# Column norms of one batch by a wide product, and ten output pairs stored singly

## The chip, the cores and the metric

The kernel runs on one core of one Trainium2 (trn2) chip. The metric is device time in microseconds (us) of one execution, as the median of several runs. The core has a matrix engine (TensorE, called PE in the profile, with its weight loads as PEld), VectorE (DVE), ScalarE (ACT), GpSimd (POOL) and a queue engine (SyncE, SP), beside sixteen DMA engines that move data between the chip's large memory (HBM) and the on-chip memory. Products of TensorE are written to PSUM, a small memory of banks that hold 512 floats in each of 128 partitions.

## The reference

There are four batches of 6400 tokens with 256 channels. In each batch the columns of q and k are scaled to length one over the tokens, a 256x256 matrix of attention between channels is formed, and v is multiplied by it. A mixture of eight rank-16 adapters with the best two per token is added to the result.

```python
def _attn_ref(q, k, v, tau):                      # q, k, v: (4, 6400, 256) float32
    qn = q / (np.linalg.norm(q, axis=1, keepdims=True) + 1e-06)
    kn = k / (np.linalg.norm(k, axis=1, keepdims=True) + 1e-06)
    s = kn.transpose(0, 2, 1) @ qn / tau
    s = s - s.max(-1, keepdims=True)
    a = np.exp(s)
    a /= a.sum(-1, keepdims=True) + 1e-09
    return v @ a

def _moe_ref(x, w_gate, A, B):                    # x: (25600, 256), 8 experts of rank 16
    logits = x @ w_gate
    topk = np.argpartition(-logits, 2, axis=1)[:, :2]
    sel = np.take_along_axis(logits, topk, axis=1)
    w = softmax(sel)                              # written out in the reference
    for e in range(8):
        for k in range(2):
            mask = topk[:, k] == e
            delta[mask] += w[mask, k, None] * (x[mask] @ A[e] @ B[e])
    return x + delta
```

## The kernel before

Each batch is cut into 50 chunks of 128 tokens, which lie in the partitions; partition p holds tokens 50p to 50p+49. q and k of a batch arrive in five stripes of ten chunks (tile `qk`, four buffers), v in stripes of 18, 16 and 16 chunks (tile `vt`, three buffers). The loads of q, k and v are issued from POOL's queue and change float32 to bfloat16 on the way; the first four chunks of q and k come through SP as float32 instead and are cast on VectorE and ScalarE. `load_more` issues the loads in one fixed order, each as soon as its buffer has been read to the end.

For a chunk, `gram` (L201) adds k-transposed times q to the bank `acc` by two products of 128x128 weights with 256 moving columns. `square` (L189) writes the squares of q and k of two chunks to a tile `sq` of 2x2x256 bfloat16 (four buffers), on ScalarE, or in batch 0 on VectorE and ScalarE in turn. `norm` (L212) sums the squares over the tokens with TensorE: for each of four blocks of 128 channels (two of q, two of k) the squares are loaded as weights and multiplied by one column of ones, so that the sums land in four columns of the bank `nrm`, one channel in each partition.

When a batch's chunks are through, `chain0` to `chain6` make its matrices: Ln and Exp on ScalarE for the root of the sums (`chain0`), the reciprocal and diagonal matrices on VectorE, a product with ones that spreads q's scales over the partitions, the product with `acc`, the exponential, transposes, and the small matrices `wa` (gate and adapters A, multiplied by the attention) and `a`.

The output is made in pairs of chunks, 25 in a batch, 100 in all (numbers u from 0): transposes of v (L341), gate logits for a group of pairs (L362), the gating steps on VectorE, the adapter products (`z_gz`, L447), `y_mm` (L463), transposes of the gated values (L471), and `delta` (L480), which adds the adapters' part (L483) and copies the pair to the tile `ys` on ScalarE (L487). A group is five pairs (the last two groups of batch 3 are three and two).

The order is written out by hand. First all of batch 0's norms and matrices; its loop takes two chunks a step, and the norms run four chunks behind the products of `gram`. All its chain steps are emitted before the first transposes of v. Then comes a loop over slots, each with one pair's work and, up to slot 67, with two or three chunks of a later batch. Stores of `ys` go out by whole groups (10 KB in a partition, 1.31 MB) and are held back: `send` keeps up to six finished groups and issues the others from ScalarE's queue, or from SP's when none is to be kept, from slot 91 on. The last five pairs are stored one by one from SP (2 KB in a partition), as the lines of `delta` say:

```python
        if u >= NPT - GRP:
            c0 = 2 * (u % NPAIR)
            nc.sync.dma_start(out_v[gr["b"], :, c0:c0 + 2, :], gr["ys"][:, r["w"]:r["w"] + 2, :])
        elif u == gr["f"] + gr["n"] - 1:
            unsent.append(gr)
```

with NPT = 100 and GRP = 5.

Of the kernel before, what the change touches and what calls it, by code (L numbers as in the profile page):

```python
# [8 lines left out]
FP32 = mybir.dt.float32  # L9
BF16 = mybir.dt.bfloat16  # L10
AX = mybir.AxisListType
OP = mybir.AluOpType
ACT = mybir.ActivationFunctionType
# [3 lines left out]
def kernel(  # L17
# [16 lines left out]
    nc = tc.nc  # L34
    B, N, C = q.shape
    P = 128
    NC = N // P
# [9 lines left out]
    NPT = B * NPAIR  # L47
    GRP = 5
# [13 lines left out]
    const = ctx.enter_context(tc.tile_pool(name="const", bufs=1))  # L62
    qk_pool = ctx.enter_context(tc.tile_pool(name="qkp", bufs=QKB))
    v_pool = ctx.enter_context(tc.tile_pool(name="vp", bufs=VB))
    sq_pool = ctx.enter_context(tc.tile_pool(name="sqp", bufs=4))
# [54 lines left out]
    def load_more(limit=1000):  # L120

        while limit and at_load[0] < len(loads):
            _, kind, b, s, parts = loads[at_load[0]]
            n = len(left[kind])
            if n >= bufs[kind] and left[kind][n - bufs[kind]]:
                return
            where[kind, b, s] = n
            c0 = s * PC if kind == "qk" else sum(VP[:s])
            left[kind].append(PC if kind == "qk" else sum(parts))
            o = left[kind][-1] - sum(parts)  # L130
            if kind == "qk":
                t = qk_pool.tile([P, 2, PC, C], BF16, tag="qk", name="qk")
            else:
                t = v_pool.tile([P, max(VP), C], BF16, tag="v", name="vt")
            tiles[kind][b, s] = t
            for m in parts:
                if kind == "qk":
                    nc.gpsimd.dma_start(t[:, 0, o:o + m, :], q_v[b, :, c0 + o:c0 + o + m, :])  # L138
                    nc.gpsimd.dma_start(t[:, 1, o:o + m, :], k_v[b, :, c0 + o:c0 + o + m, :])
                else:  # L140
                    nc.gpsimd.dma_start(t[:, o:o + m, :], v_v[b, :, c0 + o:c0 + o + m, :])
                o += m
            at_load[0] += 1
            limit -= 1
# [11 lines left out]
    nc.sync.dma_start(bst, moe_B.rearrange("e r d -> (e r) d"))  # L156
    nc.sync.dma_start(ast, moe_A.rearrange("e (p cc) r -> p e (cc r)", p=P))
    load_more(3)
    ones_bf = const.tile([P, 2], BF16)
    nc.vector.memset(ones_bf, 1.0)  # L160
    ones_f = const.tile([P, P], FP32)
    nc.vector.memset(ones_f, 1.0)
# [9 lines left out]
    ident_f = const.tile([P, P], FP32)  # L172
# [14 lines left out]
    acc, nrm, sqs = {}, {}, {}  # L187
# [24 lines left out]
    def norm(b, c):  # L212
        if c == 0:
            nrm[b] = ps_nrm.tile([P, 512], FP32, tag="nrm", name="nrm")
        sq = sqs[b, c - c % 2]
        for w in range(2):
            for ic in range(CC):
                j = w * CC + ic
                nc.tensor.matmul(  # L219
                    nrm[b][:, j:j + 1], sq[:, w, c % 2, ic * P:(ic + 1) * P], ones_bf[:, 0:1],  # L220
                    start=(c == 0 and j == 0), stop=(c == NC - 1), skip_group_check=True)
# [3 lines left out]

    def chain0(b):
        d = st.setdefault(b, {})
        lnn = bat.tile([P, 4], FP32, name="lnn")
        nc.scalar.activation(lnn, nrm[b][:, 0:4], ACT.Ln)
        rt = bat.tile([P, 4], FP32, name="rt")  # L230
        nc.scalar.activation(rt, lnn, ACT.Exp, scale=0.5)
        d["rt"] = rt
# [71 lines left out]
    def chain6(b):  # L304
        d = st[b]
        a_bf = bat.tile([P, CC, C], BF16, name="a_bf")
        for ic in range(CC):
# [3 lines left out]


    CHAIN = [(chain0, 0.0), (chain1, 0.9), (chain2, 0.75), (chain3, 0.0), (chain4, 0.55),
             (chain5, 0.65), (chain6, 0.5)]

# [164 lines left out]
    def delta(u):  # L480
        r, gr = pr.pop(u), groups[u]
        for sc in range(2):
            nc.tensor.matmul(r["y"][:, sc, :], r["gzT"][:, sc, :], ball_sb, start=False,  # L483
                             stop=(sc == 1), skip_group_check=True)
        if "ys" not in gr:
            gr["ys"] = y_pool.tile([P, 2 * GRP, C], FP32, tag="ys", name="ys")
        nc.scalar.copy(gr["ys"][:, r["w"]:r["w"] + 2, :], r["y"])  # L487
        if u >= NPT - GRP:
            c0 = 2 * (u % NPAIR)
            nc.sync.dma_start(out_v[gr["b"], :, c0:c0 + 2, :], gr["ys"][:, r["w"]:r["w"] + 2, :])  # L490
        elif u == gr["f"] + gr["n"] - 1:
            unsent.append(gr)
# [11 lines left out]
    for c in range(0, NC, 2):  # L504
        square(0, c, "act" if (c // 2) % 2 else "dve")
        gram(0, c)
        gram(0, c + 1)
        load_more()
        if c >= 4:
            norm(0, c - 4)  # L510
            norm(0, c - 3)
    for c in range(NC - 4, NC):
        norm(0, c)
# [30 lines left out]
    zq, dq = None, None  # L544
    while nz < NPT or zq is not None or dq is not None:
# [10 lines left out]
        if f in (chain0, chain1, chain2, chain3):  # L556
            f(fb)
        u = None
        if nz < min(slot, NPT) and groups[nz]["ready"]:
            u = nz  # L560
# [9 lines left out]
        if dq is not None:  # L570
            delta(dq)
        dq, zq = zq, u
# [55 lines left out]
```

## Time and profile before

| what | value |
|---|---|
| median of 3 runs (lowest, highest) | 257.0 us (256.7, 257.05) |
| the profiled execution, its own time | 256.87 us |
| its span, first to last instruction | 255.1 us |
| TensorE matmul busy | 221.0 us (87%), 3256 matmuls |
| ScalarE busy | 176.5 us (69%) |
| VectorE busy | 151.2 us (59%) |
| norm products L219 | 800, 166 ns mean of one |
| read from HBM, written to it | 78.91 MB, 26.21 MB: 412 GB/s over the span |
| clock granted to TensorE, mean over the span | 0.964 |

In a group's row the number after x is a count; then come busy time and the mean duration of one. Matmuls are pipelined, so the mean of one is longer than the distance between two. In the row of tenths a digit is the busy share of one fortieth of the span (6.4 us). In the windows the columns are the stretch, its length, busy time and count for TensorE, weight loads, VectorE, ScalarE and GpSimd, the granted clock, the mean share of the sixteen DMA engines in use, and GB/s as the DMA records count them (a load that changes float32 to bfloat16 is counted by what it writes). A bracket at the end of a timeline row is the engine's idle time before it and what ended that.

### The profile page before, as it was taken

Reading aid. Unit: us, or ns where it says so; the run is one execution under the profiler, and the core shown is the slowest. Engines: PE = TensorE matmul, PEld = TensorE weight load, DVE = VectorE, ACT = ScalarE, POOL = GpSimd, SP = SyncE. Lnnn points to the kernel's source line nnn. Section 1 sums busy time; section 2 is a strip of 40 time slices with the busy share of each in tenths; the row PEclk is TensorE's granted clock in tenths of the full one; section 3 lists DMA queues with packets and bytes.
Section 4 is the critical chain, followed back from the end, with each engine's and each line's share of the span. In section 5 each row is a group of like instructions: output and inputs, shape, how many; then the busy total and the mean of one; then the engine's idle time right before and its main releaser. Section 6 shows DMA issues by size and latency. Waiting matters only on the chain.

```text
span 255.1 us, 7688 instructions
## 1 busy us (share of the span) xinstructions
PE 221.0 (87%) x3256; PEld 194.4 (76%) x3256; DVE 151.2 (59%) x575; ACT 176.5 (69%) x290; POOL 31.6 (12%) x64
## 2 busy tenths in 40 slices
PE   0758794785899999999999989999899899999991
PEld 0546582574799987998999878989898689999980
DVE  1322244235386686775867858666577687777760
ACT  3434346448178878887788796888776867787881
POOL 8131221021012010211101202000000100000000
PEclk9999998589599999999999999999999999999999
DMA  7999999999999999999999999999999999999985
GB/s 213 223 217 217 210 216 222 208 215 216 213 221 209 216 216 214 219 211 216 216 218 211 271 277 294 220 304 260 284 259 273 372 337 351 377 423 424 418 372 226
DMA packets 13170, 66.82 MB, mean 262 GB/s; under 512 B 2512, under 2 KB 2640, under 8 KB 9296
## 3 DMA queue, kind: packets, MB, share of 16 engines
q0 software_dynamic: 8064, 38.80, 74.3%
q10 hardware_dynamic: 2160, 19.66, 18.8%
q1 hardware_dynamic: 2912, 7.87, 8.4%
q8 instruction: 25, 0.41, 0.6%
q14 instruction: 9, 0.07, 0.1%
HBM read 78.91 MB, written 26.21 MB: 412 GB/s over the span
## 4 chain that ended last, share of the span: by engine, by line
PE 48%; DMA 36%; DVE 7%; ACT 3%; POOL 2%; issue 2%; DVEq 0%; ACTq 0%; POOLq 0%
DMA qk<-in_k_dram 20%; PE y_ps L463 12%; DMA vt<-in_v_dram 11%; PE acc L207 8%; PE zg L447 6%; PE y_ps L483 6%; DMA out_dram<-ys 5%; PE vT_ps L341 5%; PE zg L471 3%; PE vT_ps L362 3%; PE nrm L219 3%; ACT sq L197 2%; DVE gz L451 2%; POOL qk L138 1%; ACT ys L487 1%
## 5 line engine op out<-in xcount | busy, mean ns | idle before, releaser
L197 ACT ACTIVATE sq<-qk 128x1024 bf16<-128x1024 bf16 x87 | 89.7, 1055 | 25.9 <-DMA qk<-in_k_dram 17.5
L207 PE MATMUL acc<-qk 128*128 128x256 bf16 x400 | 81.5, 310 | 15.2 <-DMA qk<-in_k_dram 8.8
L487 ACT COPY ys<-y_ps 128x512 f32<-128x512 f32 x100 | 58.8, 588 | 26.2 <-PE y_ps L483 22.3
L463 PE MATMUL y_ps<-a_bf,vT 128*128 128x256 bf16 x400 | 60.3, 273 | 0.9 <-ACT ys L487 0.9
L219 PEld LDWEIGHTS <-sq 128*128 128x128 bf16 x800 | 46.9, 102 | 10.1 <-ACT sq L197 3.2
L451 DVE TENSOR_TENSOR gz<-zg,gate 128x256 bf16<-128x256 f32 x100 | 41.7, 418 | 14.4 <-PE zg L447 13.0
L207 PEld LDWEIGHTS <-qk 128*128 128x128 bf16 x400 | 34.6, 106 | 20.3 <-DMA qk<-in_k_dram 10.0
L352 DVE COPY vT<-vT_ps 128x512 bf16<-128x512 bf16 x63 | 26.7, 424 | 33.2 <-PE vT_ps L341 32.5
L219 PE MATMUL nrm<-ones_bf,sq 128*128 128x1 bf16 x800 | 45.2, 166 | 1.2 <-ACT sq L197 1.2
L341 PE MATMUL vT_ps<-ident,vt 128*128 128x128 bf16 x400 | 39.8, 224 | 5.1 <-DMA vt<-in_v_dram 5.0
L447 PE MATMUL zg<-wa_sb,vT 128*128 128x128 bf16 x400 | 38.5, 219 | 1.2 <-DVE gzT L477 1.0
L483 PE MATMUL y_ps<-ball_sb,gzT 128*128 128x256 bf16 x200 | 38.4, 274 | 0.0
L463 PEld LDWEIGHTS <-vT 128*128 128x128 bf16 x400 | 33.6, 97 | 3.8 <-issue 1.0
L341 PEld LDWEIGHTS <-vt 128*128 128x128 bf16 x400 | 30.3, 100 | 8.0 <-DMA vt<-in_v_dram 5.6
L350 ACT COPY vT<-vT_ps 128x512 bf16<-128x512 bf16 x37 | 21.8, 588 | 10.2 <-PE vT_ps L341 8.7
L471 PE MATMUL zg<-ident,gz 128*128 128x128 bf16 x200 | 27.7, 220 | 1.1 <-DVE gz L451 0.6
L447 PEld LDWEIGHTS <-vT 128*128 128x128 bf16 x400 | 26.0, 97 | 3.3 <-issue 2.2
L138 POOL DMA_DIRECT2D qk<-in_q_dram x21 | 11.4, 545 | 113.7 <-ACT sq L197 31.6
L477 DVE COPY gzT<-zg 128x256 bf16<-128x256 bf16 x90 | 25.3, 281 | 0.0
L199 DVE TENSOR_TENSOR sq<-qk 128x1024 bf16<-128x1024 bf16 x13 | 9.0, 691 | 23.6 <-DMA qk<-in_k_dram 13.5
L471 PEld LDWEIGHTS <-gz 128*128 128x128 bf16 x200 | 15.2, 98 | 2.9 <-DVE gz L451 2.5
L483 PEld LDWEIGHTS <-gzT 128*128 128x128 bf16 x200 | 16.2, 98 | 0.4
(56 smaller groups left out, 152.6 us busy)
## 6 DMA issues: line engine op xcount, KB each, us to landing
out_dram<-ys ACTq DMA_DIRECT2D x15, 1280.0 KB, 12.8
qk<-in_q_dram POOLq DMA_DIRECT2D x18, 640.0 KB, 20.2
qk<-in_k_dram POOLq DMA_DIRECT2D x18, 640.0 KB, 23.6
vt<-in_v_dram POOLq DMA_DIRECT2D x7, 1024.0 KB, 27.8
out_dram<-ys SPq DMA_DIRECT2D x4, 1280.0 KB, 8.9
vt<-in_v_dram POOLq DMA_DIRECT2D x4, 1152.0 KB, 24.0
out_dram<-ys SPq DMA_DIRECT2D x5, 256.0 KB, 4.9
qk<-in_q_dram POOLq DMA_DIRECT2D x2, 384.0 KB, 12.0
```

Of the source, the lines that this page charges most:

```text
L197: nc.scalar.activation(sq, src, ACT.Square)
L207: nc.tensor.matmul(acc[b][:, ic, :], t[:, 1, o, ic * P:(ic + 1) * P], t[:, 0, o, :], start=(c == 0 and ic == 0), stop=(c == NC - 1), skip_ ...
L219: nc.tensor.matmul(nrm[b][:, j:j + 1], sq[:, w, c % 2, ic * P:(ic + 1) * P], ones_bf[:, 0:1], start=(c == 0 and j == 0), stop=(c == NC - 1 ...
L341: nc.tensor.matmul(pt[:, ic, sc * P:(sc + 1) * P], vt[:, o + sc, ic * P:(ic + 1) * P], ident, is_transpose=True, start=(i == 0), stop=(i = ...
L352: nc.vector.tensor_copy(dst, src)
L447: nc.tensor.matmul(z[:, sc, :], r["vT"][:, ic, sc, :], st[b]["wa"][:, ic, E:E + ER], start=(sc == 0 and ic == 0), stop=(sc == 1 and ic == ...
L451: nc.vector.tensor_tensor(out=gz.rearrange("p c (e r) -> p c e r", e=E), in0=z.rearrange("p c (e r) -> p c e r", e=E), in1=gr["gate"][:, r ...
L463: nc.tensor.matmul(y[:, sc, :], r["vT"][:, ic, sc, :], st[b]["a"][:, ic, :], start=(sc == 0 and ic == 0), stop=False, skip_group_check=True)
L471: nc.tensor.matmul(gt[:, sc, :], r["gz"][:, sc, :], ident, is_transpose=True, start=(sc == 0), stop=(sc == 1))
L477: nc.vector.tensor_copy(gzT, gt)
L483: nc.tensor.matmul(r["y"][:, sc, :], r["gzT"][:, sc, :], ball_sb, start=False, stop=(sc == 1), skip_group_check=True)
L487: nc.scalar.copy(gr["ys"][:, r["w"]:r["w"] + 2, :], r["y"])
```

## The change

The column of ones becomes a 128x128 tile. For batch 0 alone, `norm` uses it as the weights and streams all 512 squares of a chunk (q's 256 columns and k's 256) in one product, 50 products instead of 200. Every partition of `nrm` then holds the sums of all 512 channels. To bring them to one channel in each partition, `chain0` multiplies the bank by the identity on VectorE (the result goes to a buffer from the pool of squares) and adds up each row of 128; Ln reads these four sums. The other batches keep the four narrow products. Apart from that, pairs 90 to 94 are stored singly from SP, as 95 to 99 were before.

```diff
-    ones_bf = const.tile([P, 2], BF16)
+    ones_bf = const.tile([P, P], BF16)
     nc.vector.memset(ones_bf, 1.0)
...
         sq = sqs[b, c - c % 2]
+        if b == 0:
+
+            nc.tensor.matmul(nrm[b].rearrange("p (w d) -> p w d", w=2), ones_bf, sq[:, :, c % 2, :],
+                             start=(c == 0), stop=(c == NC - 1))
+            return
         for w in range(2):
             for ic in range(CC):
                 j = w * CC + ic
...
     def chain0(b):
         d = st.setdefault(b, {})
+        sums = nrm[b][:, 0:4]
+        if b == 0:
+            dq = sq_pool.tile([P, 4 * C], BF16, tag="sq", name="dq").bitcast(FP32).rearrange(
+                "p (j d) -> p j d", j=4)
+            nc.vector.tensor_tensor(out=dq, in0=nrm[b].rearrange("p (j d) -> p j d", j=4),
+                                    in1=ident_f[:, None, :].to_broadcast([P, 4, P]), op=OP.mult)
+            sums = const.tile([P, 4], FP32, name="sums")
+            nc.vector.tensor_reduce(out=sums, in_=dq, axis=AX.X, op=OP.add)
         lnn = bat.tile([P, 4], FP32, name="lnn")
-        nc.scalar.activation(lnn, nrm[b][:, 0:4], ACT.Ln)
+        nc.scalar.activation(lnn, sums, ACT.Ln)
...
-        if u >= NPT - GRP:
+        if u >= NPT - 2 * GRP:
             c0 = 2 * (u % NPAIR)
             nc.sync.dma_start(out_v[gr["b"], :, c0:c0 + 2, :], gr["ys"][:, r["w"]:r["w"] + 2, :])
```

## The prediction

> **What bounds the kernel now.** I read the page first (busy tenths, clock, DMA), then the chain of waits, the timeline of TensorE up to 65 us, and last the end of the span in short windows.
>
> ```profile
> span 255.1 us, 7688 instructions
> ...
> PEclk9999998589599999999999999999999999999999
> DMA  7999999999999999999999999999999999999985
> ...
> q8 instruction: 25, 0.41, 0.6%
> ```
>
> The sixteen DMA engines are at 9 tenths or more in every slice but the first and the last two: the kernel moves a fixed 105.1 MB (78.9 read, 26.2 written) and is paced by that. Slices 7 to 9 show the clock lowered. The q8 line, 25 packets, is TensorE's instruction stream, loaded through the same engines; it decides the end, as shown below.
>
> ```profile
> 5.02 24.33 DMA qk<-in_k_dram
> 36.27 28.20 DMA vt<-in_v_dram
> ...
> 184.91 13.68 DMA out_dram<-ys
> ...
> 249.62 0.59 ACT ys L487
> ```
>
> These are pieces of the chain (start, length): twice in the first 65 us it goes through a transfer that waits over 20 us in a full queue, and the last compute step is a copy at 249.6. After it only stores are left.
>
> ```profile
> 30.48 1.01 PE L207 MATMUL acc<-qk 128*128 128x256 bf16 x4
> 31.29 0.40 PE L219 MATMUL nrm<-ones_bf,sq 128*128 128x1 bf16 x8
> 31.55 1.01 PE L207 MATMUL acc<-qk 128*128 128x256 bf16 x4
> ...
> 37.04 0.60 PE L207 MATMUL acc<-qk 128*128 128x256 bf16 x4
> 37.47 0.34 PE L219 MATMUL nrm<-ones_bf,sq 128*128 128x1 bf16 x8
> 37.68 0.60 PE L207 MATMUL acc<-qk 128*128 128x256 bf16 x4
> ...
> 47.31 0.61 PE L341 MATMUL vT_ps<-ident,vt 128*128 128x128 bf16 x4 [1.88 <-DMA vt<-in_v_dram]
> ...
> 54.15 0.39 PE L207 MATMUL acc<-qk 128*128 128x256 bf16 x2 [1.01 <-DMA qk<-in_k_dram]
> ...
> 64.52 0.61 PE L341 MATMUL vT_ps<-ident,vt 128*128 128x128 bf16 x4 [3.11 <-DMA vt<-in_v_dram]
> ```
>
> A pair of chunks of batch 0 takes 31.55 - 30.48 = 1.07 us until 35 us and 37.68 - 37.04 = 0.64 after: TensorE is at half clock at first. The brackets are its waits for data: 1.88 us before the first transpose, 1.01, then 3.11; with one of 0.39 at 59.67 that is 4.5 us of waiting behind 47.3 and 6.4 in all.
>
> ```profile
> 240.00:244.00 4.00, 4.00 (x51) 3.73 (x49) 3.01 (x14) 3.42 (x10) 0.00 (x0) 1.00 0.99 411
> 244.00:246.00 2.00, 2.00 (x25) 1.83 (x23) 1.21 (x7) 1.74 (x6) 0.00 (x0) 1.00 0.67 282
> 246.00:250.00 4.00, 3.25 (x32) 2.33 (x30) 1.49 (x6) 3.16 (x9) 0.00 (x0) 1.00 0.96 392
> 250.00:252.50 2.50, 0.00 (x0) 0.00 (x0) 0.00 (x0) 0.21 (x1) 0.00 (x0) 1.00 0.99 381
> 252.50:255.10 2.60, 0.00 (x0) 0.00 (x0) 0.00 (x0) 0.00 (x0) 0.00 (x0) 0.79 0.04 16
> ```
>
> The last two numbers are DMA share and GB/s. At 244 to 246 a third of the engines idle; after 252.5 the share is 0.04 of sixteen, less than one engine. Each transfer leaves sixteen completion marks in the trace, one per engine. The last store: fifteen marks at 252.79 to 253.02, one at 254.01. The lone engine is late in all five last stores and in the two before them (249.78 against 250.90 for pairs 90 to 94, 246.73 against 247.85 for 85 to 89). Its cause is in the packet records: a q8 packet of 16 KB holds one engine for 0.88 to 0.98 us. After the first (22.5 us) one of the sixteen marks falls 0.8 us behind its neighbours, after the second (36.1) a second one, and so on to eight by 102 us; the ninth packet (107.4) puts one of those eight 2.5 us behind the first, and then the next ones. So the packets go round eight engines. Packet 25, at 243.0, is the fourth for the engine that had the 1st, 9th and 17th; the seven others have three. Marks carry no engine numbers, so it is an inference that the engines without any are those that idle at 244; the counts fit: of pairs 85 to 89 seven marks fall at 244.2 to 245.5, nine at 246.2 to 247.85.
>
> **The change part by part.** *Instructions.* 150 matmuls fewer are 150 weight loads fewer too: 300 of TensorE's 6,525 recorded instructions. Packet 1 comes after 213 of them and packet 25 after 6,394, so one every 257.5; packet 24 falls at 6,136 and packet 25 needs 6,394. The new stream has 6,225: 24 packets, eight engines with three each, and none with a fourth. The last one comes 89 instructions before the end, at about 244.7 to 245.7 by today's instruction times, on an engine that then has only two behind it. The deciding engine goes from the lone one to the group: 254.01 - 253.02 = 0.99 us less.
>
> [...]
>
> *Wide norms.* No row shows a product of 512 columns; L207's 256 columns take 0.88/4 = 0.22 us at half clock and 0.46/4 = 0.115 at full (the y rows of the chain). Twice that, two per pair: 0.88 or 0.46 us, against 0.2 for the eight narrow ones at either clock. The lower bound is the 0.2, the upper 0.88. TensorE thus gets more work: a pair takes 1.75 us at half clock, 0.89 at full. A stripe of five pairs lands every 6.3 us (16.09, 22.32, 29.35), so at half clock, 8.75 us a stripe, it would fall behind. But the clock rose at 35.6 after a stretch without idle time from 29.4 on, and its changes (35.6, 42.4, 52.6, 62.9, 69.7) lie on steps of 3.4 us; a stretch of 6.8 us without idle time holds one whole step. The stripe begun at 22.4 reaches that by 29.2 at the latest. From there at 0.89: its rest by 30.2, the next stripe by 34.6, the last by 39.1, and four chunks of norms left over, 4 x 0.23: 40.0 at worst, against 38.85 now. If warm earlier, the end is set by the last landing at 35.6 and 38.9 to 39.5 comes out.
>
> *Diagonal and sum on VectorE before Ln.* The product over 128x512 has rows at 0.24 us for 80 elements and 0.42 for 256 (L393, L451): 0.68 for 512 on that line; the reduction has 0.23 for 80 (L389), so about 0.7. Bounds for both: 0.84 (twice the 256 row) to 1.68 (four times); I take 1.4. Behind the Ln, ScalarE has batch 0's own steps and the first squares of batch 1, which TensorE and a load of POOL wait for. Batch 0's matrices, at 45.6 today, come 1.4 to 2.6 us later. The cover is the wait of 1.88 for the first v stripe and then the 4.5 us of waits behind: at most 0.7 us spills over and is gone by 64.5. Without that cover it would cost the whole 2.6. Loads are issued later by as much; those issued at 21.96 to 42.1 land 17 to 28 us after their issue, so the queue doesn't run dry. Front: 0. The memset, the one tile taken from the pool of squares: 0, both are done beside loads.
>
> *Stores.* Five more pairs go out singly, each right after its copy (241.1 to 245.07) instead of together at 245.09. SP issues four more, 0.33 to 0.44 us each, about 1 us apart; nothing but stores is behind them. The third of the engines that idles gets work, but every engine writes its own eight rows, so the eight loaded ones, busy without a gap, gain nothing. They pay: rows of 2 KB instead of 10 KB. Bounds: the lone engine took 3.05 us for pairs 90 to 94 and 3.1 for the five singles (+0.06); the fifteen took 3.05 and then 3.24 by their last marks, 3.40 by their first (+0.35). I take 0.25, nearer the second, as the loaded engines still run together. A gain is excluded on them by the absence of idle time. The last copy doesn't take over: its store issued at 250.24 needs 0.85 to its first packet, 0.67 of rows and 0.35 to the mark (as the 245.09 store shows on an idle engine): 252.1.
>
> [...]
>
> **Sum.** The profiled run took 256.87 us for a span of 255.1, 0.13 under the median of 257.0. -0.99 + 0.25 + 0 = -0.74: 256.13 on the profiled run, 256.25 on the median. The likeliest case's own range is 256.0 to 256.5 (-1.0 to -0.5).
>
> **Rivals.** *The straggler stays* (another packet falls late on a loaded engine, or the packets go round otherwise). For it: packet 24 does come near the end. Against it: the regular round of eight. Then only the rows count, +0.06 to +0.35: 257.1 to 257.4.
>
> *Slower: TensorE stays at half clock through batch 0.* 20 pairs from 16.1 at 1.75 end at 51.1, with the norms left over at 52.9, 14 us later than now, and 15.6 with VectorE's steps. It decides from 6.4 us on, the waits that cover it: 9 us remain at 64.5. Behind that TensorE's idle time from 80 to 200 (4.0 us by the windows) and 0.9 at the end absorb some: +4, 261. A milder form is any TensorE delay of over 7 us. Against it: the clock rose under a busy stretch of 6.2 us, and wide products leave no gaps.
>
> *Larger gain: the filled idle time counts.* If engines shared rows, 7 engines times 2 us over 16 would give 0.9 more: 255.3. The sixteen marks per transfer speak against it.
>
> *Not what it says:* "fewer matmuls" doesn't relieve TensorE, whose batch-0 time grows by 25 x 0.25 = 6 us or more; it relieves the instruction stream.
>
> **How the numbers follow.** A measurement of this kernel can tell about 0.2% from no change: below 256.49 is faster, above 257.51 slower. Forecast 0.60 (0.06 of it above 256.49), straggler 0.20, slower 0.15, larger gain 0.05. Faster 0.54 + 0.05 = 0.59, same 0.06 + 0.20 = 0.26, slower 0.15. The range 255.9 to 257.4 holds the forecast and the straggler, and leaves out the other two, 0.20.
>
> **What would show it.** Right: q8 with 24 packets; the last store's sixteen marks within 0.5 us, near 253.3; a DMA share near 0.9 at 244 to 246; batch 0's Ln 1.5 to 2.6 us later and the transpose at 64.5 where it was. Wrong: 25 packets or a lone late mark; TensorE late at 64.5; a last copy later than 250; gaps in DMA before 240.

## The result and the profile after

The changed kernel takes 256.25 us (median of 8 runs, 256.15 to 256.43) where the kernel before takes 256.94 (8 runs, 256.70 to 257.17): a ratio of 0.9976, 95% interval 0.9967 to 0.9986, faster by 0.69 us. The forecast was 256.25, 0.75 less than before. The profiled execution took 256.33 us with a span of 254.5 (before: 256.87 and 255.1). Of two runs below, `stores_only` and the first `spare50`, the profiled execution was disturbed; only their times are used.

The page of the changed kernel, the rows that answer to those of before:

```profile
span 254.5 us, 7398 instructions
...
PEclk9999998589599999999999999999999999999996
DMA  7999999999999999999999999999999999999995
...
q8 instruction: 24, 0.39, 0.6%
```

There is one packet less in TensorE's instruction stream, and DMA is as full as before. The chain of waits, in its longer pieces:

```profile
1.90 7.97 DMA qk<-in_k_dram
...
16.49 19.26 DMA qk<-in_k_dram
36.03 28.47 DMA vt<-in_v_dram
...
248.38 0.59 ACT ys L500
```

It goes through the same kind of full queue, and the last copy comes at 248.4 instead of 249.6. TensorE's timeline:

```profile
11.60 1.06 PE L207 MATMUL acc<-qk 128*128 128x256 bf16 x4
12.45 1.06 PE L218 MATMUL nrm<-sq,ones_bf 128*128 128x512 bf16 x2
13.30 1.06 PE L207 MATMUL acc<-qk 128*128 128x256 bf16 x4
...
17.05 0.60 PE L207 MATMUL acc<-qk 128*128 128x256 bf16 x4
17.49 0.59 PE L218 MATMUL nrm<-sq,ones_bf 128*128 128x512 bf16 x2
17.92 0.60 PE L207 MATMUL acc<-qk 128*128 128x256 bf16 x4
...
47.41 0.61 PE L354 MATMUL vT_ps<-ident,vt 128*128 128x128 bf16 x4 [0.83 <-DMA vt<-in_v_dram]
...
53.50 0.39 PE L207 MATMUL acc<-qk 128*128 128x256 bf16 x2 [0.38 <-DMA qk<-in_k_dram]
...
59.71 0.39 PE L207 MATMUL acc<-qk 128*128 128x256 bf16 x2 [1.08 <-DMA qk<-in_k_dram]
...
64.54 0.61 PE L354 MATMUL vT_ps<-ident,vt 128*128 128x128 bf16 x4 [3.16 <-DMA vt<-in_v_dram]
```

A pair of chunks costs 13.30 - 11.60 = 1.70 us at half clock and 17.92 - 17.05 = 0.87 at full clock. The full clock comes at 14.9 us, not at 35.6 (the first records of the granted clock in the two traces are a 1.0 at 14.92 and at 35.56). At 64.5 TensorE is where it was: the waits at 47.4 and 53.5 have become shorter, the one at 59.7 longer (1.08 instead of 0.39), and the last one is as it was. Behind the norms stand the two new steps on VectorE and then Ln on ScalarE:

```profile
38.70 0.69 DVE L237 TENSOR_TENSOR dq<-nrm,ident_f 128x512 f32<-128x512 f32 x1 [2.14 <-PE nrm L218]
39.43 0.69 DVE L240 TENSOR_REDUCE sums<-dq 128x4 f32<-128x512 f32 x1
...
40.15 0.20 ACT L242 ACTIVATE lnn<-sums 128x4 f32<-128x4 f32 x1 [3.24 <-DVE sums L240]
```

Before, Ln came at:

```profile
38.89 0.17 ACT L229 ACTIVATE lnn<-nrm 128x4 f32<-128x4 f32 x1 [1.20 <-PE nrm L219]
```

The end, with the same columns as in the windows before:

```profile
240.00:244.00 4.00, 4.00 (x51) 3.71 (x49) 3.07 (x15) 3.58 (x9) 0.00 (x0) 1.00 1.00 414
244.00:246.00 2.00, 2.00 (x24) 1.71 (x22) 1.04 (x7) 1.82 (x6) 0.00 (x0) 1.00 0.92 368
246.00:250.00 4.00, 2.00 (x19) 1.32 (x16) 0.70 (x2) 2.18 (x5) 0.00 (x0) 1.00 0.97 371
250.00:252.50 2.50, 0.00 (x0) 0.00 (x0) 0.00 (x0) 0.00 (x0) 0.00 (x0) 0.59 0.70 269
252.50:254.50 2.00, 0.00 (x0) 0.00 (x0) 0.00 (x0) 0.00 (x0) 0.00 (x0) 0.50 0.02 8
```

The idle third at 244 to 246 is filled (0.67 to 0.92), but what is filled there goes missing at 250 to 252.5 (0.99 to 0.70): engines that are not loaded finish early and the loaded ones still set the end. The last store's marks: six at 250.85 to 251.05, ten at 252.07 to 253.19, the last two 0.13 apart. No engine is late alone any more. Ten late marks are two more than the eight engines that the prediction calls loaded; the two at 252.07 and 252.48 lie apart from the other eight (252.74 and later). The trace has a second instruction queue, q14, with nine packets of 8 KB in the span, 0.31 to 0.32 us each, which could be what two more engines carry; no mark names its engine, so this is not shown.

### The profile page after: what moved, and what is told of

Same layout as the page of the kernel before. It is cut to its first block, busy times and chain, and to the rows that moved or that the text cites. A ratio compares the mean times of both kernels' runs of the same rounds, so it can differ in the third digit from the quotient of the medians.

```text
span 254.5 us, 7398 instructions
## 1 busy us (share of the span) xinstructions
PE 220.9 (87%) x3106; PEld 190.1 (75%) x3106; DVE 152.6 (60%) x577; ACT 176.3 (69%) x290; POOL 31.6 (12%) x64
## 4 chain that ended last, share of the span: by engine, by line
PE 62%; DMA 22%; DVE 8%; ACT 3%; issue 2%; POOL 1%; DVEq 0%; POOLq 0%; ACTq 0%
PE y_ps L476 16%; DMA vt<-in_v_dram 11%; PE acc L207 11%; DMA qk<-in_k_dram 11%; PE zg L460 8%; PE y_ps L496 7%; PE vT_ps L354 7%; PE zg L484 4%; PE nrm L224 4%; PE vT_ps L375 4%; DVE gz L464 2%; ACT sq L197 1%; DVE e L406 1%; ACT ys L500 1%; DVE lm L410 1%
## 5 line engine op out<-in xcount | busy, mean ns | idle before, releaser
L207 PE MATMUL acc<-qk 128*128 128x256 bf16 x400 | 74.9, 288 | 14.0 <-DMA qk<-in_k_dram 7.5
L224 PEld LDWEIGHTS <-sq 128*128 128x128 bf16 x600 | 36.4, 98 | 7.4 <-ACT sq L197 3.1
L224 PE MATMUL nrm<-ones_bf,sq 128*128 128x1 bf16 x600 | 35.9, 165 | 1.2 <-ACT sq L197 1.2
L476 PEld LDWEIGHTS <-vT 128*128 128x128 bf16 x400 | 33.6, 97 | 3.5 <-issue 0.7
L496 PEld LDWEIGHTS <-gzT 128*128 128x128 bf16 x200 | 16.1, 98 | 0.4
## 6 DMA issues: line engine op xcount, KB each, us to landing
out_dram<-ys SPq DMA_DIRECT2D x10, 256.0 KB, 5.3
```

The lines of the kernel that those rows point to most:

```text
L207: nc.tensor.matmul(acc[b][:, ic, :], t[:, 1, o, ic * P:(ic + 1) * P], t[:, 0, o, :], start=(c == 0 and ic == 0), stop=(c == NC - 1), skip_ ...
L224: nc.tensor.matmul(nrm[b][:, j:j + 1], sq[:, w, c % 2, ic * P:(ic + 1) * P], ones_bf[:, 0:1], start=(c == 0 and j == 0), stop=(c == NC - 1 ...
L476: nc.tensor.matmul(y[:, sc, :], r["vT"][:, ic, sc, :], st[b]["a"][:, ic, :], start=(sc == 0 and ic == 0), stop=False, skip_group_check=True)
```

## The experiments

The main theory: the gain is one instruction packet, and the stores cost a little. The rivals: the stores gain by filling idle engines; or the wide products gain, by the early clock and what comes earlier with it. Each kernel was timed in five rounds, kernels of a group together on one chip. The changed kernel itself came out at 256.25 and, in the third group, at 256.47, so medians of different groups are comparable to about 0.2 us; within a group the ratio to the kernel before counts.

### First group: the two edits apart, and the stream apart from both

`norms_only`: the change without its store edit.

```diff
-        if u >= NPT - 2 * GRP:
+        if u >= NPT - GRP:
```

> The wide norms of batch 0 without the store edit. Stream theory (the gain is the 25th instruction packet of TensorE, which made one DMA engine late; the singles cost a little): 24 packets, no lone late mark in the last store, and without the cost of five more single pairs: 0.99 us under the kernel before, 255.9 to 256.1, span near 254.1. Store theory (the gain comes from filling the idle third of the engines at 244 to 246 us): no gain, 256.8 to 257.1.

Measured: 256.0 us, ratio 0.9959 (0.9945 to 0.9972); 24 packets, last marks of the last store 252.98 and 253.19. All of the gain and more.

`stores_only`: the kernel before with the store edit alone.

```diff
-        if u >= NPT - GRP:
+        if u >= NPT - 2 * GRP:
```

> The kernel before with pairs 90 to 94 stored singly, norms as before. Stream theory: 25 packets and one mark of each of the last stores about 1 us behind the other fifteen; time 0.06 to 0.35 us over the kernel before, 257.0 to 257.3. Store theory: 256.2 to 256.4, the whole gain of the change.

Measured: 257.22, ratio 1.0007 (0.9998 to 1.0016). The store theory falls; that the edit costs something is likely, but the interval holds 1.

`fewer_norms`: the kernel before; in batch 0 the norms of three chunks in four are left out, which shortens TensorE's stream without any wide product.

```diff
         sq = sqs[b, c - c % 2]
+        if b == 0 and c % 4:
+            return
...
-                    start=(c == 0 and j == 0), stop=(c == NC - 1), skip_group_check=True)
+                    start=(c == 0 and j == 0), stop=(c == NC - 1 or (b == 0 and c == NC - 2)), skip_group_check=True)
```

> The kernel before, narrow norms, stores as before, but batch 0's norms are summed over every fourth chunk alone (13 of 50), which leaves 148 products and 148 weight loads out of the stream (6,229). No wide product, no steps on VectorE, no early clock by wide products. Stream theory: 24 packets, no lone late mark, 0.99 us less: 255.9 to 256.1. Rival (wide products and the early clock make the gain): 256.8 to 257.1.

Measured: 256.09, ratio 0.9960 (0.9947 to 0.9972), 24 packets, last marks 253.00 and 253.20. A shorter stream alone, with narrow norms, gives the gain of the wide norms. A pair of batch 0 costs TensorE less time here than before (at full clock 34.62 - 33.64 = 0.98 us for two pairs, 0.49 each, against 0.64) and more in `norms_only`, which has the wide products of the changed kernel (0.87 there), and both gain the same.

`spare150`: the changed kernel with three spare narrow products per chunk.

```diff
                              start=(c == 0), stop=(c == NC - 1))
+            if c == 0:
+                st["spare"] = ps_y.tile([P, 2, C], FP32, tag="y", name="spare")
+            for j in range(3):
+                nc.tensor.matmul(st["spare"][:, 0, j:j + 1], sq[:, j // 2, c % 2, (j % 2) * P:(j % 2 + 1) * P],
+                                 ones_bf[:, 0:1], start=True, stop=True, skip_group_check=True)
             return
```

> The changed kernel with three spare narrow products for each chunk of batch 0 (150 products and 150 weight loads into a bank that is otherwise unused then; nothing reads them), so that TensorE's stream has again 6,525 recorded instructions. All else of the change stays: the wide norms, the early full clock, the steps on VectorE, the singles. Stream theory: 25 packets, a lone late mark again; the changed kernel's time plus 0.9: 257.0 to 257.4. Rival (the gain comes from the early clock, or from loads and the last copy that come earlier): as the changed kernel, 256.2 to 256.4.

Measured: 257.39, ratio 1.0011 (1.0002 to 1.0019). The wide norms, the early clock (full at 13.1 us, lowered again from 30.1 to 33.6) and the singles are all there and the gain is gone. The DMA row for the stream and the window behind 252.5, of `spare150` and then of `norms_only`:

```profile
q8 instruction: 25, 0.41, 0.6%
...
252.50:256.00 3.50, 0.00 (x0) 0.00 (x0) 0.00 (x0) 0.00 (x0) 0.00 (x0) 0.50 0.06 22
```

```profile
q8 instruction: 24, 0.39, 0.6%
...
252.50:256.00 3.50, 0.00 (x0) 0.00 (x0) 0.00 (x0) 0.00 (x0) 0.00 (x0) 0.65 0.01 4
```

With 25 packets the thin tail is back (22 GB/s against 4; a share of 0.06 of sixteen is about one engine), and so is the lone mark: 253.30 for the last of fifteen, 254.48 for the sixteenth.

### Steps, not slopes

`spare50`, `spare100` and `spare300` have `range(1)`, `range(2)` and `range(6)` in that loop (the six take their weights from the four blocks in turn).

> The changed kernel with one spare narrow product per chunk of batch 0 instead of three: 100 instructions more than the changed kernel (6,325 recorded), still short of the 6,394 at which the 25th packet comes. Stream theory: a step, not a slope: 24 packets, no lone late mark, the changed kernel's time, 256.1 to 256.4. Rival (each spare product costs time on TensorE): a third of what the 150 cost, 256.5 to 256.8.

> The kernel with one spare product per chunk again, for its trace and beside the changed kernel. It was 256.53, between the two theories. Step theory: 24 packets, no mark of the last store alone by a microsecond, within 0.3 of the changed kernel. Slope theory: a late engine or a later last copy that explains 0.3 to 0.5 more.

> Two spare products per chunk, 6,425 recorded instructions, 31 more than the 6,394 at which the 25th packet was issued in the kernel before. Step theory: the 25th packet comes just before the end, at 248 to 249 us, and makes its engine late: 257.1 to 257.5, near the kernel with 150. Slope theory: halfway between 50 and 150, 256.9 to 257.0.

> The same with six spare products per chunk, 6,825 recorded instructions: 26 packets, the 26th on a second engine, so that two engines have four packets and none five. Stream theory: as with 150, since the two are late at the same time: 257.2 to 257.6. Rival (time in proportion to packets or to TensorE's work): twice the step of 150, 258.2 to 258.8.

| spare products | recorded instructions | packets | median us | ratio to before (95%) | last two marks of the last store |
|---|---|---|---|---|---|
| 0 (`after_again`) | 6,224 | 24 | 256.47 | 0.9980 (0.9971 to 0.9989) | 253.08, 253.20 |
| 50 (`spare50`) | 6,324 | 24 | 256.53 | 0.9980 (0.9971 to 0.9989) | not used |
| 50 (`spare50_again`) | 6,324 | 24 | 256.48 | 0.9982 (0.9973 to 0.9990) | 253.43, 253.46 |
| 100 (`spare100`) | 6,424 | 25 | 257.47 | 1.0022 (1.0013 to 1.0031) | 253.47, 254.19 |
| 150 (`spare150`) | 6,524 | 25 | 257.39 | 1.0011 (1.0002 to 1.0019) | 253.30, 254.48 |
| 300 (`spare300`) | 6,824 | 26 | 257.51 | 1.0021 (1.0012 to 1.0030) | 254.32, 254.35 |

The third group's repeat of the changed kernel had this expectation:

> The changed kernel once more, so that the three kernels beside it are compared with it on one chip: 256.15 to 256.45.

The traces record one instruction fewer than the expectations count (6,224 for the changed kernel instead of 6,225); nothing hangs on it. Fifty products cost nothing, the next fifty a microsecond, the 200 after them nothing. `spare50` at 256.53 lay inside the slope theory's numbers; beside the changed kernel on one chip (256.48 and 256.47) that reading falls. In `spare300` the two last marks are 0.03 apart: two engines are late together, at the price of one. The page rows of `spare50_again` and `spare100`, one packet apart:

```profile
q8 instruction: 24, 0.39, 0.6%
```

```profile
q8 instruction: 25, 0.41, 0.6%
```

### The stores

The traces of the first group showed a cost that I had not counted. SP ends the program by waiting for the eight semaphores that its and ScalarE's stores use in turn, in a fixed order, 0.06 us each. What SP waited for at the end (us in total, number of waits, the longest), before and then after the change:

```profile
SPq L623 <- DMA out_dram<-ys: 3.1, 5, 0.8
```

```profile
SPq L636 <- DMA out_dram<-ys: 3.8, 1, 3.8
```

Before, five waits end with a landing each and three follow the last one. After, one wait of 3.8 us takes all of it: it is for the last store, which stands first in the order, and seven more follow. The trace shows them one by one: before, SP passes the wait that the last landing ends at 254.03 and the three others at 254.09, 254.15 and 254.21; after, it passes the eight from 253.21 to 253.64. From the last mark to the span's end it is 255.1 - 254.01 = 1.09 us before and 254.5 - 253.19 = 1.31 after.

`singles15`: five more pairs singly (`NPT - 3 * GRP`).

> The changed kernel with fifteen pairs stored singly instead of ten. Rows theory (my prediction: five more singles cost 0.06 to 0.35 by their 2 KB rows): 256.3 to 256.6. End theory, formed from the traces of the first runs: the rows cost nothing, and the store edit costs at the very end, where SP waits for the eight semaphores of the stores in a fixed order, 0.06 us each; ten singles put the last transfer on the first of the eight (seven waits follow, 0.43), five put it on the fifth (three follow, 0.19), and fifteen put it there again: 0.24 less than the changed kernel, 255.9 to 256.1.

Measured: 256.31, ratio 0.9974 (0.9964 to 0.9983): the rows theory's number. In the trace 254.4 - 253.34 = 1.06 lie behind the last mark, 0.25 less than in the changed kernel, with five waits that end with a landing as before the change:

```profile
SPq L636 <- DMA out_dram<-ys: 3.0, 5, 0.6
```

The end theory was right on the order of the waits. The last mark at 253.34 is 0.15 later than in the changed kernel, which would be the rows; but the other kernels with ten singles and 24 packets have it at 253.20 (`after_again`) to 253.51 (`sums_thrice`), so a cost of the rows is not shown by it.

`nine_stores`: pairs 90 and 91 in one transfer.

```diff
-        if u >= NPT - 2 * GRP:
-            c0 = 2 * (u % NPAIR)
-            nc.sync.dma_start(out_v[gr["b"], :, c0:c0 + 2, :], gr["ys"][:, r["w"]:r["w"] + 2, :])
+        if u == NPT - 2 * GRP:
+            return
+        if u > NPT - 2 * GRP:
+            n = 4 if u == NPT - 2 * GRP + 1 else 2
+            c1, w1 = 2 * (u % NPAIR) + 2, r["w"] + 2
+            nc.sync.dma_start(out_v[gr["b"], :, c1 - n:c1, :], gr["ys"][:, w1 - n:w1, :])
```

> The changed kernel with pairs 90 and 91 stored by one transfer, so that the last ten pairs take nine transfers. Rows theory: 0.01 to 0.07 less than the changed kernel, 256.2. End theory: the last transfer is then on the last of the eight semaphores, no wait follows it, 0.43 less than the changed kernel and 0.19 less than with the wide norms and five singles: 255.7 to 255.9, under both kernels.

Measured: 255.97, ratio 0.9955 (0.9943 to 0.9968), with 254.2 - 253.29 = 0.91 behind the last mark. That is 0.07 above the end theory's range and 0.2 under the rows theory's number. Six waits end with a landing, the last of them with the last store, and none follows:

```profile
SPq L639 <- DMA out_dram<-ys: 3.6, 6, 0.6
```

Zero, three and seven waits behind it go with 0.91, 1.06 to 1.11 (`norms_only`: 254.3 - 253.19) and 1.31. This kernel and `norms_only` (256.0) are both under the changed one by their medians, but the intervals of both still meet its first one (0.9967 to 0.9986), and nothing parts the two from each other.

### The cover of batch 0's chain

`sums_thrice`: the two new steps on VectorE three times.

```diff
-            nc.vector.tensor_tensor(out=dq, in0=nrm[b].rearrange("p (j d) -> p j d", j=4),
-                                    in1=ident_f[:, None, :].to_broadcast([P, 4, P]), op=OP.mult)
             sums = const.tile([P, 4], FP32, name="sums")
-            nc.vector.tensor_reduce(out=sums, in_=dq, axis=AX.X, op=OP.add)
+            for _ in range(3):
+                nc.vector.tensor_tensor(out=dq, in0=nrm[b].rearrange("p (j d) -> p j d", j=4),
+                                        in1=ident_f[:, None, :].to_broadcast([P, 4, P]), op=OP.mult)
+                nc.vector.tensor_reduce(out=sums, in_=dq, axis=AX.X, op=OP.add)
```

> The changed kernel with the product with the identity and the row sums on VectorE made three times instead of once: batch 0's matrices come 2.8 us later. Cover theory (as predicted: 0.83 us of wait are left before the first transpose and 4.6 behind it, so that TensorE goes on at 64.5 as before): no change, within 0.15 of the changed kernel. Rival (the chain of batch 0 is on the path): 2.8 us more, 259.0.

Measured: 256.62, ratio 0.9983 (0.9974 to 0.9992), 0.15 over the changed kernel beside it. TensorE's waits for data in its timeline:

```profile
59.93 0.39 PE L207 MATMUL acc<-qk 128*128 128x256 bf16 x2 [0.43 <-DMA qk<-in_k_dram]
...
64.76 0.40 PE L355 MATMUL vT_ps<-ident,vt 128*128 128x128 bf16 x4 [3.16 <-DMA vt<-in_v_dram]
```

The waits at 47 and 53 us are used up, the one at 59.9 is shorter than the changed kernel's 1.08, and the 3.16 before 64.8 is untouched. 2.9 us more on the chain (four steps of 0.69 with their gaps) are hidden.

## Why the prediction was right

The mechanism was right in its main term. That the median meets the forecast of 256.25 to the hundredth is chance: the forecast for the profiled execution was 256.13 and it took 256.33, and the repeat of the changed kernel had a median of 256.47.

*The stream, -0.99: right in mechanism and close in size.* 24 packets as counted, no lone mark. The last mark went from 254.01 to 253.19, -0.82: the lone engine's -0.99, and +0.17 because the last of the others came at 253.19 instead of 253.02. It did so in `norms_only` too, without the store edit; what moved it is open. By their ratios `norms_only` and `fewer_norms` gained 1.05 and 1.03 us. Packet 24 came at 243.5 us, a microsecond before the predicted time. Not every packet shows in the time: the 25th cost about 1 us (257.47 in `spare100` against 256.48 in `spare50_again`) because it made a single engine the last, the 26th nothing that the runs could tell (257.51 in `spare300`).

*The stores, +0.25: near the measured difference of medians, in part by luck, as a term was missing.* I put it all on the 2 KB rows. `norms_only` and the changed kernel end with the same last mark (253.19), `singles15` 0.15 later: by the last marks the rows cost 0 to 0.15 for five singles, no more than single executions differ. The packet records would give more: a 2 KB row holds its engine for 0.084 us and a 10 KB row for 0.39, so as an estimate five singles cost each engine 40 x 0.084 - 8 x 0.39 = 0.24 us; why the last marks don't show that is open. What the traces do show is 0.22 more behind the last landing, seven waits instead of three, which I had not looked for, though the three of before were in the trace. The difference between the changed kernel and `norms_only` is 0.25 us by medians and 0.0017 by ratios (0.44 us), with overlapping intervals, so the size of the whole term is not settled better than that. The number of transfers costs little here: after the change the last marks of the last eight singles lie 0.63 to 0.66 us apart, about what eight rows of 0.084 us take (0.67), and four more transfers with their smaller rows and the waits behind them move the time by these 0.25 to 0.44 us.

*The front, 0: right.* The wide products were priced at 1.75 and 0.89 us a pair and took 1.70 and 0.87. The two steps on VectorE were priced at 0.68 and 0.7 and took 0.69 each. The clock rose earlier than my worst case (14.9 against 29.2), so the norms ended no later than before (38.6 against 38.9) and Ln came at 40.15 instead of 38.89, 1.26 later, a little under the 1.5 to 2.6 given. All of it went into the waits, as `sums_thrice` shows with room to spare. The 6.3 us between stripes in the prediction fit its first two landings alone; from 22.32 to 29.35 it is 7.0, and the sum does not change by it.

*The signs.* Packets, DMA share and the transpose at 64.5 were as given. Wrong: sixteen marks within 0.5 us. The unloaded engines now run ahead, and the spread is 2.3; the sign should have been the distance of the last mark from the one before it.

*Rivals.* The slow rival fell with the clock at 14.9, the store gain with `stores_only`. Not predicted and not settled: the last copy came 1.24 us earlier. With 25 packets it is 0.5 earlier (249.1 in `spare150`), and the loaded engines end after it in any case.

## What to carry to other kernels

Look at the marks of the last transfers one by one. Here, with the mean DMA share at 9 tenths or more in all but the first and the last two slices, the one engine with the most to move set the end: its mark came at 254.01, the fifteen others by 253.02. A lone late mark named a load that the mean share hid (0.04 of sixteen behind 252.5), and here it was the program's own instructions. They came in blocks of 16 KB, one for about 257 recorded instructions, so the time moved in steps: 256.47 and 256.48 us with 6,224 and 6,324 instructions, 257.47 with 6,424. A cut within a block paid nothing, the one that crossed it a microsecond at once; and only the block that made the first engine late counted, as the 26th packet, at 257.51, cost nothing that the runs could tell. Count also what the program waits for behind its last landing: the order of these waits and the number of transfers before them moved the end by 0.4 us (0.91 us behind the last mark with no wait left, 1.31 with seven).

## What the runs showed of the hardware

- TensorE's instructions came in packets of 16 KB, one for about 257 recorded instructions (before the 1st came after 213 and the 25th after 6,394, after the change the 24th after 6,137); each held one DMA engine for 0.88 to 0.98 us before and after the change, and they went round eight of the sixteen engines by the count of late marks before (eight by 102 us, then one of these later still, by 2.5 us behind the first); the two late marks with 26 packets (254.32 and 254.35) agree. Why it is eight no run here tests.
- The full clock came at 13.1 to 15.7 us in the ten profiled executions with wide products used here, at 35.6 and 31.9 us in those of the kernel before and `fewer_norms`. How long TensorE works without a wait does not explain this by itself: after the change the clock rose in a stretch from 9.9 to 15.1 us, and before it two longer ones, 16.1 to 21.6 and 22.4 to 27.9, passed without a rise. Counted in the steps of 3.4 us that the prediction found, the stretch after the change holds the whole step that ends at 14.9, and the two before hold none (the nearest runs from 18.5 to 21.9); the first whole one before ends at 35.6. So where the stretches fall against the steps seems to count. It is not settled: a step with matmuls in 90% of it raised the clock in `spare150`, the 18.5 to 21.9 before, with 92%, did not, and no run varies the position alone.
- SP's waits at the program's end cost 0.06 us each (253.21 to 253.64 for the seven that follow the first after the change), and those behind the last landing are the ones that showed in the time: with none, three and seven of them 0.91, 1.06 to 1.11 and 1.31 us lie behind the last mark.
